# A tuned cross-network kernel: all weights kept in DRAM as 4 KB rows and loaded through the GpSimd queue

## The chip, the cores and the metric

The kernel runs on one core of one Trainium2 chip. The metric is the device time in microseconds (us). A core has TensorE (matmul), VectorE, ScalarE, GpSimd and SyncE; in the profile they are PE, DVE, ACT, POOL and SP, and "SPq" or "POOLq" is the queue of transfers that the engine issues. The profile counts 16 DMA engines for the core, and gives the time of each queue's packets as a share of all 16: in the kernel before 49.0% for q1, the queue of SyncE, and 14.4% for q0, that of GpSimd.

## The reference

```python
B, Din, L = 16384, 1024, 6            # x0 [B, 1024], ws [6, 1024, 1024], bs [6, 1024], bf16
def reference(x0, ws, bs):
    x = x0
    for l in range(L):
        x = x0 * (x @ ws[l] + bs[l]) + x      # written with einsum in the original
    return x
```

## The kernel before

The batch is cut into 8 passes (`lp`) of 2048 rows. A pass runs the 6 layers, and each layer runs two lanes of 1024 rows, so there are 96 "units" of one pass, one layer and one lane. While TensorE works on one lane, VectorE prepares the other. The product of a unit is computed with a seven-product (Strassen-like) scheme on quarters of the matrices, which needs sums of weight quarters. Pass 0 builds those sums on VectorE and saves them in a DRAM tile `Lc`; passes 1 to 7 load nine 512 KB weight tiles per layer into a ring of ten, six from `Lc` (a 4 KB row per partition) and three from the input `ws` (1 KB rows). That makes 7 x 6 x 9 = 378 loads, 252 from `Lc` and 126 from `ws`.

Activations are held transposed. So at a pass boundary three kinds of transfer meet, for each of four quarters of each lane: `x0L` of the next pass is loaded by a DMA transpose from DRAM, the result `xf` goes through a DMA transpose in SBUF back to row order (into `xL`), and `xL` is stored. In the kernel before, these and all the weight loads are issued by SyncE, on one queue.

```python
RING = 10
CIDX = {5: 0, 6: 1, 7: 2, 3: 3, "2i": 4, "4i": 5}
Lc = dram.tile([L, len(CIDX), P, KH * H], BF16, name="Lc")

def w_src(l, pid):                       # where a weight tile [128, 4, 512] comes from
    wl = ws[l]
    if pid == 1:
        return wl[0:H, 0:H].rearrange("(k p) e -> p k e", p=P)
    ...                                  # pid 2 and 4: other quarters of ws
    return Lc[l, CIDX[pid]].rearrange("p (k e) -> p k e", k=KH)

def prefetch():                          # called at every step; loads as far as ring slots are free
    while st["next"] < len(keys) and can_alloc(st["next"]):
        key = keys[st["next"]]
        if key[0] == 0 and key[2] not in (1, 2, 4):
            return
        t_ = alloc_next(key)
        st["dma"] = nc.sync.dma_start(t_[:], w_src(key[1], key[2]))

def combo(l, pid):                       # pass 0 only
    ...
    nc.sync.dma_start(Lc[l, CIDX[pid]].rearrange("p (k e) -> p k e", k=KH), t_[:])

def load_x0(lp, lane, eh, n):
    r0 = lp * LB + lane * PR + n * NB
    nc.sync.dma_start_transpose(out=q(x0L[lane], eh, n), in_=x0[r0:r0 + NB, eh * H:(eh + 1) * H])

def store_quarter(lp, lane, eh, n, xf):
    ...
    nc.sync.dma_start_transpose(out=dst, in_=xf[:].rearrange("r j k p -> r (j k p)"))
    nc.sync.dma_start(out[r0:r0 + NB, eh * H:(eh + 1) * H].rearrange("(j p) d -> p j d", p=P),
                      q(xL[lane], eh, n).rearrange("p j d -> p j d"))

def x_out(c, eh, n):
    if last_layer:
        xf = late["xf"].tile([P, KH, KH, P], BF16, name="xf")      # a pool of two buffers
        tt(xf[:]..., c..., q(xst, eh, n)..., ADD)                  # VectorE, cut
        store_quarter(lp, lane, eh, n, xf)
    elif l > 0:
        nc.gpsimd.dma_start(q(xst, eh, n), c, accum_op=ADD)
    else:
        tt(q(xst, eh, n), c, q(x0T, eh, n), ADD)

def finish(c, add, eh, n):
    tt(c, c, add, ADD)
    tt(c, c, q(x0T, eh, n), MULT)
    if nxt_x0:                                     # last layer, and a next pass exists
        load_x0(lp + 1, lane, eh, n)
    x_out(c, eh, n)
```

The `xf` pool has two buffers, so the third `xf` on VectorE must wait until the transpose of the first has landed. And the ring's slots come free in units of lane 1, so the nine loads for the first layers of the next pass are issued during the last unit of a pass, just when the boundary's transposes run.

## Time and profile before

| | before |
|---|---|
| time, median of 3 runs (range) | 2414.31 us (2412.28 to 2418.68) |
| span of the profiled run, mean granted clock | 2414.6 us, 0.983 |
| a unit inside a pass, TensorE without a gap | 23.38 us |
| the first three units of a pass, over 3 x 23.38 us (mean of seven) | 17.2 us |

The last row was worked out from the trace: a unit starts where ScalarE first evicts its P1 product. Seven boundaries of 17.2 us are 120 us, the largest loss in a kernel whose TensorE is otherwise full.

The page's busy time (busy us, share of the span, instructions), and the shares of the chain that ended last:

```profile
PE 2286.9 (95%) x12912; PEld 1269.5 (53%) x12912; DVE 2116.1 (88%) x2096; ACT 1783.9 (74%) x2485; POOL 110.7 (5%) x133
...
PE 77%; DVE 15%; DMA 5%; SPq 1%; issue 1%; ACT 1%; DVEq 0%; ACTq 0%
```

The transfers of before, from the page (out<-in, queue, kind, count, KB each, median us from issue to landing):

```profile
wp<-Lc SPq DMA_DIRECT2D x252, 512.0 KB, 4.6
wp<-in_ws_dram SPq DMA_DIRECT2D x139, 512.0 KB, 5.9
...
x0L<-in_x_dram SPq DMA_TRANSPOSE x64, 5.4
```

The waits of before (engine and line, what it waited for: us in total, times, longest):

```profile
DVE xf L63 <- DMA xL<-xf: 95.4, 21, 8.6
...
PE XB L259 <- DMA wp<-Lc: 45.5, 12, 5.9
PE XB L259 <- DMA wp<-in_ws_dram: 18.3, 7, 7.8
```

TensorE's waits for weights are the inviting target. The chain of waits tells another story. Here is the third boundary of before (start us, us, what), which has no weight load in it:

```profile
917.36 2.30 DVE D L63
...
919.69 1.24 DVE xf L63
920.93 2.49 SPq L150
...
923.52 5.08 DMA xL<-xf
928.60 0.02 issue
928.62 1.22 DVE xf L63
929.85 0.08 DVE Q L63
929.92 7.32 DMA x0L<-in_x_dram
...
951.98 1.02 PE XA L247 x4
```

VectorE's multiply at 917.36 frees `x0L` of lane 1; the transposes into it are issued only at 929.92, because the sync queue is still busy. That queue's own timeline of before shows with what:

```profile
917.10 0.46 SPq L100 DMA_DIRECT2D wp<-in_ws_dram  x1
917.65 5.76 SPq L150 DMA_TRANSPOSE x0L<-in_x_dram  x1
923.52 3.04 SPq L155 DMA_TRANSPOSE xL<-xf  x1
926.68 0.98 SPq L100 DMA_DIRECT2D wp<-Lc  x2
928.62 0.39 SPq L156 DMA_DIRECT2D out_dram<-xL  x1
929.43 0.39 SPq L100 DMA_DIRECT2D wp<-in_ws_dram  x1
929.92 6.67 SPq L150 DMA_TRANSPOSE x0L<-in_x_dram  x2
```

And the stretches around this boundary, with busy time of each engine, granted clock, DMA share and GB/s:

```profile
core 0: us, PE busy (x) PEld busy (x) DVE busy (x) ACT busy (x) POOL busy (x), PEclk, DMA share, GB/s
885.00:905.00 20.00, 20.00 (x118) 11.35 (x116) 12.25 (x11) 15.75 (x23) 0.00 (x0) 1.00 1.06 201
905.00:925.00 20.00, 14.45 (x75) 7.28 (x74) 15.61 (x18) 9.99 (x14) 0.00 (x0) 0.91 1.18 294
925.00:945.00 20.00, 14.81 (x78) 7.96 (x76) 13.33 (x14) 10.36 (x15) 0.00 (x0) 0.83 1.05 261
```

### The profile page before, as it was taken

What the parts mean: (1) busy time and instruction counts of PE and PEld (TensorE: products, weight loads), DVE (VectorE), ACT (ScalarE), POOL (GpSimd) and SP (SyncE); (2) the same over time, 40 slices, a digit from 0 to 9 for tenths busy, and PEclk for the clock granted to TensorE, in tenths of its full rate; (3) what the DMA queues carried; (4) which work ended last, traced back from release to release, by engine and by line L of the source; (5) the groups of instructions that cost most, each with busy time, mean ns of one, the idle gap of its engine ahead of it and who ended that gap; (6) DMA issues with size and microseconds to landing.
All of it is one profiled execution on the core that took longest, in us unless ns stands there. A gap on an engine that the chain in (4) does not pass through costs nothing.

```text
span 2414.6 us, 32963 instructions
## 1 busy us (share of the span) xinstructions
PE 2286.9 (95%) x12912; PEld 1269.5 (53%) x12912; DVE 2116.1 (88%) x2096; ACT 1783.9 (74%) x2485; POOL 110.7 (5%) x133
## 2 busy tenths in 40 slices
PE   6999989999899997999989999899998999989997
PEld 3454545555455554555545555455554555545553
DVE  6998879998899988999879998799987999889997
ACT  4777767777677785787767887677776878768775
POOL 0000000000000000000000000000000000000000
PEclk9999999999999999999999999999999999999998
DMA  7465695557954579545784558845588456874566
GB/s 200 137 188 136 161 236 139 148 131 179 240 150 126 135 183 237 147 122 147 191 230 130 131 149 197 218 126 131 153 201 222 114 136 165 208 197 123 147 172 144
DMA packets 439899, 400.10 MB, mean 166 GB/s; under 512 B 276416, under 2 KB 386496, under 8 KB 439744
## 3 DMA queue, kind: packets, MB, share of 16 engines
q1 hardware_dynamic: 421312, 330.89, 49.0%
q0 software_dynamic: 18432, 67.12, 14.4%
q8 instruction: 101, 1.65, 0.3%
q14 instruction: 54, 0.44, 0.1%
HBM read 211.29 MB, written 52.43 MB: 109 GB/s over the span
## 4 chain that ended last, share of the span: by engine, by line
PE 77%; DVE 15%; DMA 5%; SPq 1%; issue 1%; ACT 1%; DVEq 0%; ACTq 0%
PE pA L247 35%; PE XA L247 23%; PE XB L259 19%; DVE t L63 4%; DVE D L63 3%; DVE ti L63 3%; DMA xL<-xf 3%; DMA x0L<-in_x_dram 2%; DVE S L63 2%; SPq L150 1%; DVE xf L63 1%; DVE xL L63 1%; DVE Q L63 1%; ACT P5s L239 1%; DMA wp<-in_ws_dram 0%
## 5 line engine op out<-in xcount | busy, mean ns | idle before, releaser
L247 PEld LDWEIGHTS <-wp 128*128 128x128 bf16 x7712 | 759.0, 99 | 773.8 <-issue 46.6
L247 PE MATMUL pA<-t,wp 128*128 128x512 bf16 x3104 | 780.2, 381 | 0.0
L259 PEld LDWEIGHTS <-wp 128*128 128x128 bf16 x5040 | 494.9, 99 | 333.8 <-DMA wp<-Lc 51.3
L239 ACT CAST F<-XB 128x1024 bf16<-128x1024 f32 x360 | 364.3, 1012 | 291.0 <-PE XB L259 284.4
L259 PE MATMUL XB<-ti,wp 128*128 128x256 bf16 x2880 | 436.9, 275 | 52.4 <-DMA wp<-Lc 45.5
L247 PE MATMUL XA<-t,wp 128*128 128x512 bf16 x1536 | 400.6, 385 | 2.4 <-DMA wp<-Lc 2.4
L247 PE MATMUL XA<-xL,wp 128*128 128x512 bf16 x1280 | 326.8, 379 | 2.3 <-ACT P5s L239 2.3
L247 PE MATMUL pA<-xL,wp 128*128 128x512 bf16 x1280 | 328.5, 379 | 0.0
L242 ACT ACTIVATE U3s<-pA,b_all 128x512 bf16<-128x512 f32 x384 | 264.4, 688 | 39.4 <-PE pA L247 19.0
L239 ACT CAST G<-XB 128x512 bf16<-128x512 f32 x360 | 211.7, 588 | 106.5 <-PE XB L259 105.2
L242 ACT ACTIVATE P1s<-pA,b_all 128x512 bf16<-128x512 f32 x384 | 266.0, 693 | 26.3 <-PE pA L247 18.5
L242 ACT ACTIVATE U2s<-pA,b_all 128x512 bf16<-128x512 f32 x384 | 266.1, 693 | 14.4 <-PE pA L247 5.1
L239 ACT CAST S<-XA 128x1024 bf16<-128x1024 f32 x192 | 194.3, 1012 | 64.1 <-PE XA L247 64.1
L239 ACT CAST P5s<-XA 128x1024 bf16<-128x1024 f32 x192 | 195.3, 1017 | 50.1 <-DVE D L63 30.8
L63 DVE TENSOR_TENSOR D<-D,x0L 128x4096 bf16<-128x4096 bf16 x96 | 220.0, 2292 | 13.3 <-ACT D L242 9.4
L63 DVE TENSOR_TENSOR t<-xL 128x4096 bf16<-128x4096 bf16 x80 | 183.4, 2293 | 23.4 <-DMA xL<-S 14.7
L63 DVE TENSOR_TENSOR t<-xL,t 128x2048 bf16<-128x2048 bf16 x160 | 194.9, 1218 | 0.0
L63 DVE TENSOR_TENSOR xL<-D,xL 128x4096 bf16<-128x4096 bf16 x64 | 146.7, 2292 | 6.6
L63 DVE TENSOR_TENSOR S<-S,U2s 128x2048 bf16<-128x2048 bf16 x96 | 117.2, 1221 | 31.8 <-ACT S L239 31.5
L305 POOL DMA_DIRECT2D xL<-Q x64 | 55.2, 863 | 1905.9 <-ACT U3s L242 862.2
L259 PE MATMUL XB<-t,wp 128*128 128x256 bf16 x1008 | 139.3, 275 | 0.0
L63 DVE TENSOR_TENSOR D<-P5s,U3s 128x2048 bf16<-128x2048 bf16 x96 | 117.3, 1222 | 24.4 <-ACT U3s L242 24.4
(43 smaller groups left out, 1752.0 us busy)
## 6 DMA issues: line engine op xcount, KB each, us to landing
wp<-Lc SPq DMA_DIRECT2D x252, 512.0 KB, 4.6
wp<-in_ws_dram SPq DMA_DIRECT2D x139, 512.0 KB, 5.9
xL<-Q POOLq DMA_DIRECT2D x64, 512.0 KB, 5.7
xL<-S POOLq DMA_DIRECT2D x64, 512.0 KB, 6.4
out_dram<-xL SPq DMA_DIRECT2D x64, 512.0 KB, 3.8
Lc<-wp SPq DMA_DIRECT2D x36, 512.0 KB, 5.0
w<-in_ws_dram SPq DMA_DIRECT2D x12, 512.0 KB, 7.7
x0L<-in_x_dram SPq DMA_TRANSPOSE x64, 5.4
```

What stands on the lines that cost most here:

```text
L63: return nc.vector.tensor_tensor(out=out, in0=in0, in1=in1, op=op)
L150: nc.sync.dma_start_transpose(out=q(x0L[lane], eh, n), in_=x0[r0:r0 + NB, eh * H:(eh + 1) * H])
L239: nc.scalar.copy(out=dst, in_=src)
L242: nc.scalar.activation(out=dst, in_=src, func=IDENT, bias=bias_col(eh, m), scale=1.0)
L247: nc.tensor.matmul(dst, lhsT=w_[:, k, m * P:(m + 1) * P], rhs=b_[:, k, :], start=(start and k == 0), stop=(k == KH - 1), skip_group_check= ...
L259: nc.tensor.matmul(dst[:, m * NQ:(m + 1) * NQ], lhsT=wv[:, k, m * P:(m + 1) * P], rhs=b_[:, k, :], start=(start and m == 0 and k == 0), st ...
L305: nc.gpsimd.dma_start(q(xst, eh, n), c, accum_op=ADD)
```

## The change

The intent: the sync queue should carry only input and output. All nine weight tiles of a layer are kept in DRAM in the load's own layout, one 4 KB row per partition, and passes 1 to 7 load them through GpSimd's queue, which has little else to do (POOL is busy 5% of the span before). Pass 0 gains 18 saves. The whole diff, with context cut:

```diff
-    CIDX = {5: 0, 6: 1, 7: 2, 3: 3, "2i": 4, "4i": 5}
+    CIDX = {5: 0, 6: 1, 7: 2, 3: 3, "2i": 4, "4i": 5, 1: 6, 2: 7, 4: 8}
     Lc = dram.tile([L, len(CIDX), P, KH * H], BF16, name="Lc")
 ...
-        return Lc[l, CIDX[pid]].rearrange("p (k e) -> p k e", k=KH)
+        raise KeyError(pid)
+
+    def w_save(l, pid, t_):
+        nc.sync.dma_start(Lc[l, CIDX[pid]], t_[:].rearrange("p k e -> p (k e)"))
 ...
             t_ = alloc_next(key)
-            st["dma"] = nc.sync.dma_start(t_[:], w_src(key[1], key[2]))
+            if key[0] == 0:
+                nc.sync.dma_start(t_[:], w_src(key[1], key[2]))
+                if key[2] in (1, 2):
+                    w_save(key[1], key[2], t_)
+            else:
+                nc.gpsimd.dma_start(t_[:].rearrange("p k e -> p (k e)"), Lc[key[1], CIDX[key[2]]])
 ...
         nc.sync.dma_start(w22[l][:], w_src(l, 4))
+        w_save(l, 4, w22[l])
 ...
-        nc.sync.dma_start(Lc[l, CIDX[pid]].rearrange("p (k e) -> p k e", k=KH), t_[:])
+        w_save(l, pid, t_)
 ...
     t_ = alloc_next((0, 0, 1))
     nc.sync.dma_start(t_[:], w_src(0, 1))
+    w_save(0, 1, t_)
```

## The prediction

> **What bounds the kernel now.** TensorE is busy 2286.9 of 2414.6 us (page, part 1). By the timeline, a layer-and-lane unit inside a batch pass takes exactly 23.38 us without a TensorE gap; two hold 44.4 us of VectorE work (windows). The 96 units would so take about 2250 us; the rest is the start (first matmul at 11.1 us), the tail (about 17 us) and seven pass boundaries, each about 17 us over (first unit 35 to 39 us, second 24 to 28, third 24.1).
>
> At a boundary TensorE's visible gaps are mostly waits for weights, about 10 us each time, then 0.4 to 3.4 us for P5s, and the granted clock falls to 0.5 for 3.4 to 13.7 us. [...] But the chain of waits gives weight loads 0%. At 903 us it runs: VectorE 902.8 to 919.7 without a gap; then the x0 transposes for lane 1, whose input is free at 919.7, are issued only at 929.9, because SyncE is still issuing an earlier transpose (5.8 us), then a result transpose, weights, and a store that waits for a landing; x0 lands at 937.3; VectorE to 950.7; P5s; TensorE at 952.0. So weight waits lie mostly in the shadow of the SyncE/VectorE chain.
>
> **What changes.** TensorE, VectorE, ScalarE keep their order. 378 weight loads (252 from Lc, 126 from ws) move to GpSimd; SyncE loses them, gains 18 saves. GpSimd issues cost 0.86 us each (measured on its accumulates): no limit. 1 KB rows become 4 KB rows, but 512 KB takes each of the 16 engines 1.66 us in 1 KB packets (52 ns) and 1.6 us in 4 KB (199 ns): almost nothing. [...] the trace shows them at a share of 1.0 or more from 885 to 945 us. Bandwidth is not gained, only order.
>
> - Boundary gain: weights are issued when a slot frees (887 to 904 us) instead of 903 to 930. Weight gaps go. Lane 1's x0 transposes issue about 8 to 10 us earlier.
> - Loss there: up to six weight loads (1.6 us each) now compete with the transposes of 885 to 905 us, which hold VectorE (6.0 us wait): estimated 3 us later.
> - Net 7 us a boundary, 49 in all.
> - Start: the saves of the first two weights wait for landings (4.9, 6.3 us) ahead of the x0 transposes issued at 2.3: plus 5 us.
> - Mid-pass: [...] VectorE waits only 0.4 us for these accumulates. Unchanged.
>
> **Prediction: 2370 us** (-1.8%), range 2330 to 2420. Faster by over 2%: 0.42; within 2%: 0.54; slower: 0.04.
>
> **Right or wrong by:** waits of TensorE for weights from about 70 us to under 15; stretches at clock 0.5 mostly gone; first unit of a pass near 30 us, with waits for P5s or x0 in place of weights; wait of lane 1's x0 transposes after their input is free from 10 us to about 2; first matmul near 14 us; inner units still 23.38.
>
> **What would make it wrong:** the transposes slowed far more by competing weights (no gain); accumulates delayed behind weights so that VectorE falls behind in every unit (slower); or a chain that shortens fully, towards 2300.

The forecast's sum: 49 us won at the boundaries less 5 us lost at the start is 44 us, from 2414 to 2370.

## The result, and the profile after

| | before | after |
|---|---|---|
| time, median (range), 4 runs each | 2413.72 us (2412.28 to 2418.68) | 2509.32 us (2500.48 to 2515.29) |
| ratio of fast runs, 95% interval | | 1.0389 (1.0352 to 1.0427) |
| mean granted clock of the profiled run | 0.983 | 0.957 |

A ratio is the mean time of one kernel's fast runs over that of the other's fast runs of the same rounds, so it is not quite the ratio of the medians quoted beside it. The changed kernel is 3.9% slower. It computes the right result.

The page after shows the same amount of matmul, VectorE and ScalarE work in a longer span, and more DMA in the chain:

```profile
PE 2288.3 (91%) x12912; PEld 1272.6 (51%) x12912; DVE 2115.3 (84%) x2096; ACT 1784.9 (71%) x2485; POOL 314.4 (13%) x511
...
PE 76%; DVE 13%; DMA 7%; SPq 2%; ACT 1%; issue 1%; DVEq 0%; ACTq 0%
```

The transfers after. The median of a transpose has hardly moved, which hides what happened:

```profile
wp<-Lc POOLq DMA_DIRECT2D x378, 512.0 KB, 6.2
...
x0L<-in_x_dram SPq DMA_TRANSPOSE x64, 5.2
xL<-xf SPq DMA_TRANSPOSE x64, 4.6
```

The times from issue to landing, taken one by one from the two traces:

| us to landing | before: median / 90% / longest | after: median / 90% / longest |
|---|---|---|
| x0L<-in_x_dram | 5.5 / 8.6 / 9.3 | 5.2 / 25.5 / 31.5 |
| xL<-xf | 4.5 / 5.3 / 6.2 | 4.6 / 15.3 / 24.3 |

The medians of the first table and of this one differ by 0.1 us in one place because landings are matched singly here. A tenth of the `x0L` transposes, those at boundaries, now take 25 us and more. The waits after:

```profile
DVE xf L63 <- DMA xL<-xf: 215.7, 16, 35.4
...
PE XB L269 <- DMA x0L<-in_x_dram: 91.2, 6, 23.6
...
PE XB L269 <- DVE ti L63: 56.5, 8, 14.3
PE XA L257 <- ACT P5s L249: 23.2, 9, 3.8
...
PE XB L269 <- DMA wp<-Lc: 14.4, 1, 14.4
```

By these lines the weight waits of TensorE are nearly gone, as intended. In their place it waits for `x0L` transposes and for VectorE's `ti`, which is made from them. But a wait is put down to what came last, and the loads do not land early: at this boundary the last of them and the transpose land 0.02 us apart, and the weight-load unit (PEld) waits for `wp` three times in the run, 54.6 us in all. The chain of the same boundary after is one long step:

```profile
935.30 0.86 PE pA L257 x4
...
936.18 20.40 DMA xL<-xf
...
957.82 2.28 DVE t L63
...
972.42 1.86 PE XA L257 x4
```

The sync queue of after, in the same stretch, holds nothing but transposes and stores. Here one line can cover several issues (x2):

```profile
924.46 0.38 SPq L165 DMA_DIRECT2D out_dram<-xL  x1
924.92 11.15 SPq L159 DMA_TRANSPOSE x0L<-in_x_dram  x2
936.18 20.41 SPq L164 DMA_TRANSPOSE xL<-xf  x2
```

Over the whole run a single issue of a transpose on SyncE took up to 20.6 us (median 2.8); before it was 6.7 at most (median 2.4).

And this is what GpSimd's timeline after has at that time: nine weight loads between 923.90 and 939.92, of which three are shown.

```profile
923.90 0.53 POOL L108 DMA_DIRECT2D wp<-Lc  x1 [29.30 <-PE pA L257]
925.20 0.53 POOL L108 DMA_DIRECT2D wp<-Lc  x1 [0.77 <-PE XB L269]
...
939.92 0.53 POOL L108 DMA_DIRECT2D wp<-Lc  x1 [0.34 <-PE pA L257]
```

Matched to landings: the second `x0L` transpose, issued at 929.65, landed at 954.80 (25.2 us), and the first `xf` transpose, issued at 936.18, landed at 956.58 (20.4 us). The last of the nine loads landed at 954.8. The transposes ended when the loads ended. The stretches of after (columns as before) show TensorE almost empty for 20 us while the DMA engines are counted full and move no more bytes than in the stretch ahead of it:

```profile
921.00:941.00 20.00, 19.49 (x111) 10.57 (x108) 7.34 (x7) 16.45 (x24) 4.76 (x9) 1.00 1.09 215
941.00:961.00 20.00, 1.26 (x6) 0.76 (x7) 4.29 (x4) 0.21 (x1) 0.00 (x0) 0.57 1.10 217
961.00:981.00 20.00, 16.20 (x72) 7.95 (x71) 18.30 (x21) 8.83 (x12) 0.00 (x0) 0.75 0.95 213
```

**Where the 95.6 us are.** Four measures from the traces place them:

| mean of seven boundaries, us | before | after | difference |
|---|---|---|---|
| first three units of a pass, over 3 x 23.38 | 17.2 | 30.9 | +13.7 |
| start of lane 1's first `xf` on VectorE, after the start of the last unit | 18.5 | 42.8 | +24.3 |
| VectorE's wait just ahead of it, for an `xL<-xf` transpose | 5.3 | 29.5 | +24.2 |
| from that `xf` to the landing of lane 1's last x0 transpose | 37.9 | 26.2 | -11.7 |

Seven times 13.7 us is 96 us, the loss (the start adds 1.7 us; the two profiled runs themselves differ by 98.6). Units inside a pass are 23.38 us in both. So two things happened at each boundary. The part that the change was made for seems to come out as hoped: 11.7 us were won from lane 1's `xf` on. But 24.3 us were lost ahead of it, waiting for the transposes of lane 0. The two are not independent: by the time of lane 1's `xf` the loads had all landed, and in h1 below, where the delay is gone and the loads run beside lane 1's transposes, the 11.7 us are gone too. TensorE's idle time also went with a lower granted clock: up to the last matmul, 64.9 us at half clock before, 198.0 us after.

### The profile page after: what moved, and what is told of

Same layout as the page of the kernel before. It is cut to its first block, busy times and chain, and to the rows that moved or that the text cites. A ratio compares the mean times of both kernels' runs of the same rounds, so it can differ in the third digit from the quotient of the medians.

```text
span 2513.2 us, 33038 instructions
## 1 busy us (share of the span) xinstructions
PE 2288.3 (91%) x12912; PEld 1272.6 (51%) x12912; DVE 2115.3 (84%) x2096; ACT 1784.9 (71%) x2485; POOL 314.4 (13%) x511
## 4 chain that ended last, share of the span: by engine, by line
PE 76%; DVE 13%; DMA 7%; SPq 2%; ACT 1%; issue 1%; DVEq 0%; ACTq 0%
PE pA L257 35%; PE XA L257 23%; PE XB L269 18%; DMA xL<-xf 6%; DVE t L63 3%; DVE D L63 3%; DVE ti L63 2%; DVE S L63 2%; SPq L159 2%; DVE Q L63 1%; DVE xL L63 1%; DVE xf L63 1%; DMA x0L<-in_x_dram 0%; ACT P5s L249 0%; ACT P1s L252 0%
## 5 line engine op out<-in xcount | busy, mean ns | idle before, releaser
L108 POOL DMA_DIRECT2D wp<-Lc x378 | 219.3, 614 | 1156.3 <-PE pA L257 836.8
L63 DVE TENSOR_TENSOR xf<-Q,xL 128x2048 bf16<-128x2048 bf16 x16 | 19.6, 1225 | 206.9 <-DMA xL<-xf 206.6
```

The lines of the kernel that those rows point to most:

```text
L63: return nc.vector.tensor_tensor(out=out, in0=in0, in1=in1, op=op)
L108: nc.gpsimd.dma_start(t_[:].rearrange("p k e -> p (k e)"), Lc[key[1], CIDX[key[2]]])
```

## The experiments

The theories, with the letters that some expectations use:

- **A.** The weight loads share the DMA engines with the transposes, and another queue's packets take turns with the transposes' packets. A weight packet in the trace has 4096 bytes and takes about 159 ns, a transpose packet 256 bytes and about 18 ns. In a turn-by-turn service the transposes get little. A1: taking turns is all of it. A2: sharing also loses throughput.
- **B.** It is something special to GpSimd's queue.
- **C.** It is the order of issue alone: the loads come earlier, whatever their packets are.
- **D.** It is the layout: the 4 KB rows or the 18 saves.
- **L** (formed later, when A1 did not give the size): the sync queue feeds the 16 DMA engines in step, so the engines that also serve a foreign load set the pace for all.

### 1. e1_sync_4k: the layout alone

The changed kernel, with its loads back on the sync queue.

```diff
-                nc.gpsimd.dma_start(t_[:].rearrange("p k e -> p (k e)"), Lc[key[1], CIDX[key[2]]])
+                nc.sync.dma_start(t_[:].rearrange("p k e -> p (k e)"), Lc[key[1], CIDX[key[2]]])
```

> All weights saved as 4 KB rows as in the change, but loaded by the sync queue again. Theories: A, the DMA engines take turns packet by packet between two queues, so that a transpose of 256 B packets gets one packet through for each 4 KB packet of weights on the other queue; [...] C, the bytes of the weights merely come earlier than the transposes, whatever the queue and the packet; D, the 4 KB rows themselves are bad. A, B and C expect the time of before within 1% (2395 to 2430 us), with first units of 35 to 39 us and weight waits of TensorE near 70 us again; D expects over 2480.

Measured: 2420.73 us median against 2416.47, ratio 1.0022 (1.0005 to 1.0038). The boundary excess is 17.0 us, as before. The layout neither costs nor wins at boundaries; D is out.

### 2. e2_gp_1k: 1 KB rows on GpSimd's queue

The changed kernel, with `Lc` laid out so that a load reads 1 KB rows.

```diff
-    Lc = dram.tile([L, len(CIDX), P, KH * H], BF16, name="Lc")
+    Lc = dram.tile([L, len(CIDX), KH, P, H], BF16, name="Lc")
 ...
-        nc.sync.dma_start(Lc[l, CIDX[pid]], t_[:].rearrange("p k e -> p (k e)"))
+        nc.sync.dma_start(Lc[l, CIDX[pid]].rearrange("k p e -> p k e"), t_[:])
 ...
-                nc.gpsimd.dma_start(t_[:].rearrange("p k e -> p (k e)"), Lc[key[1], CIDX[key[2]]])
+                nc.gpsimd.dma_start(t_[:], Lc[key[1], CIDX[key[2]]].rearrange("k p e -> p k e"))
```

> The change with the saved weights laid out so that each packet is 1 KB, still on the GpSimd queue. A: a transpose packet now waits behind a 1 KB packet (46 to 52 ns) and not a 4 KB one (159), so the slowest transposes at a boundary land in about 12 us and not in 25, and the kernel takes 2430 to 2475 us. B and C expect 2495 to 2525 as the change. D expects 2400 to 2430.

Measured: 2527.66 us (2514.97 to 2551.64), ratio 1.0475 (1.0412 to 1.0539). As a test of packet size it failed, for a reason that the trace shows: GpSimd's queue has 64,768 packets of 4096 bytes, the same count as in the changed kernel. The 1 KB rows were merged into 4096-byte packets, so the packet size of the change was never altered. Its ratio is 0.9% above that of the change, but the two intervals overlap, so that it is slower than the change is not shown.

### 3. e3_gp_only: the queue alone

The kernel before, with nothing changed but the queue of the loads of passes 1 to 7.

```diff
-            st["dma"] = nc.sync.dma_start(t_[:], w_src(key[1], key[2]))
+            (nc.sync if key[0] == 0 else nc.gpsimd).dma_start(t_[:], w_src(key[1], key[2]))
```

> The queue alone: the kernel before with its weight loads of later passes on the GpSimd queue, two thirds of them in 4 KB packets and one third in 1 KB, no saves of 1, 2 and 4. A: nearly the change, 2470 to 2510 us. B and C: 2495 to 2525 less the 2 us of the start. D: 2400 to 2430.

Measured: 2504.1 us (2484.63 to 2508.65), ratio 1.0351 (1.0309 to 1.0393). The same wait as in the changed kernel appears:

```profile
DVE xf L63 <- DMA xL<-xf: 211.6, 15, 34.5
```

The queue alone gives nine tenths of the loss (3.51% of 3.89%, and the intervals overlap). With e1, the two halves of the change are told apart. One thing came with the queue: here too GpSimd's queue has 64,768 packets of 4096 bytes, so the third of the loads that comes from `ws` in 1 KB rows was merged, and the expectation's mix of packets was not what ran.

### 4. e4_act_4k: the loads on ScalarE's queue

```diff
-                nc.gpsimd.dma_start(t_[:].rearrange("p k e -> p (k e)"), Lc[key[1], CIDX[key[2]]])
+                nc.scalar.dma_start(t_[:].rearrange("p k e -> p (k e)"), Lc[key[1], CIDX[key[2]]])
```

> The change with the weight loads issued by ScalarE: another queue than the transposes', 4 KB packets[...]. A and C: as the change, 2490 to 2530 us, transposes at a boundary of 20 to 25 us. B: 2420 or less. ScalarE spends 0.3 to 0.5 us an issue, nine in two units in which it has 9 us free, so inner units should stay at 23.4 us.

Measured: 2490.86 us (2484.5 to 2492.8), ratio 1.0307 (1.0289 to 1.0324). The run is confounded, because ScalarE's evictions stood behind its issues of loads: at 1237.26 us the issue of two loads took 17.32 us, and the next eviction began at 1254.63. Two waits show what that cost; the issue of a load held ScalarE up, and with it TensorE:

```profile
ACT U3s L252 <- DMA out_dram<-xL: 74.0, 6, 17.6
...
PE XB L269 <- ACT G L249: 69.5, 6, 16.8
```

Still, transposes were slow here too: 16.7 us at the longest for `x0L`, 18.0 for `xL<-xf`. So slow transposes are not special to GpSimd's queue, which weakens B. The time itself decides nothing: the loss lies in the last unit of a pass, 42.7 to 52.6 us long instead of 23.38, where ScalarE stood.

### 5. m1_phases: bursts of transposes and loads by themselves

A micro-kernel. Its output is wrong, which doesn't matter for the time. Each phase issues a few transposes on the sync queue and as many 512 KB loads on some queue, all at once, and VectorE then waits for all of them.

```python
def tp(i):       # transpose of [512, 512] from DRAM, sync queue
    nc.sync.dma_start_transpose(out=T[i][:], in_=x0[i * NB:(i + 1) * NB, 0:H])
def w4(q, i):    # 512 KB load in 4 KB rows, on queue q (w1: 1 KB rows, w256: 256 B rows)
    q.dma_start(W[i][:], Ld[i])
for i in range(4): (tp(i), w4(gp, i))
sync_all()
for i in range(4): (tp(i), w4(sp, i))
sync_all()
...              # more phases
```

> The disputed cost by itself; wrong results on purpose, the time of the whole says nothing. Phases, each ended by a barrier, of four 512 KB transposes on the sync queue, four 512 KB loads, or both. From the kernels' traces an undisturbed transpose should take 2.2 to 2.8 us of the DMA engines and a 4 KB-row load 1.3 to 1.6, so four of each alone about 13 and 9 us with the first landing, and together, if engines lose nothing by mixing them, 17 to 20 us. C (order alone): together on two queues as long as alternating on one queue, within 2 us, whatever queue and packet. A1 (taking turns, packet by packet, without loss): the sum of both stays at 17 to 20 us, but the transposes land last, after all 4 KB loads; with 256 B rows on the other queue the transposes land earlier. A2 (transposes beside another queue lose throughput): together on two queues over 25 us, on one queue 17 to 20. B [...]: slow with GpSimd, not with ScalarE's queue. Two plain loads on two queues: no loss under any of these. The eight-and-eight phases should show the same twice as large.

Landing times from the start of the phase, from the trace:

| phase | transposes land at, us | loads land at, us |
|---|---|---|
| 4 loads, GpSimd, alone | | 3.6 to 8.3 |
| 8 transposes alone | last 20.3 | |
| 4 + 4, GpSimd 4 KB | 6.4, 11.7, 14.3, 16.2 | 4.9, 7.3, 8.8, 10.2 |
| 4 + 4, all on the sync queue, alternating | 3.8, 8.7, 12.7, 16.6 | last 18.4 |
| 4 + 4, ScalarE 4 KB | 15.0, 16.8, 18.9, 20.9 | 3.6 to 15.2 |
| 4 + 4, ScalarE 1 KB | 7.8, 12.4, 14.6, 16.5 | 4.8, 7.8, 9.6, 11.4 |
| 4 + 4, ScalarE 256 B | 7.0, 11.3, 15.4, 19.4 | 6.6, 11.1, 15.2, 19.2 |
| 4 + 4, GpSimd 1 KB rows (merged to 4096 B, as in e2) | first 8.4, last 17.1 | |
| 8 + 8, GpSimd 4 KB | 5.7, then 17.1 to 29.4 | last 16.0 |
| 8 + 8, all on the sync queue | last 34.0 | |

Transposes alone need about 2.1 us each, so nothing is lost in total: 8 + 8 takes 29.4 us on two queues and 34.0 on one. But the loads come first. In the 8 + 8 phase, while both were going, the trace counts 144 weight packets against 161 transpose packets in the 1.5 us from 246.7: nearly one to one. One for one is 4096 bytes against 256. On ScalarE's queue the landings follow the row size: with 256-byte rows both sides land together (the last at 19.4 and 19.2 us), with 4096-byte rows the first transpose lands at 15.0 us. C, order alone, cannot give this dependence on the rows; B is not needed. A1 holds for bursts and A2 does not. Three more phases fit: beside GpSimd's stores the transposes landed at 6.6 to 16.4 us; transposes within SBUF beside GpSimd's loads landed at 10.3 to 18.4; and eight plain loads on two queues took 13.7 us, about 1.7 each, so nothing was lost.

The changed kernel's trace shows the same at the boundary: 125 weight packets to 142 transpose packets in the 1.5 us from 945.5, and 124 to 140 from 947.0. Transposes alone have 1200 to 1600 packets in that time. These are the stretches with most weight packets; the others look different (see m2).

### 6. e5_store_gp: another transfer beside the transposes

The kernel before, with only the output stores on GpSimd's queue.

```diff
-        nc.sync.dma_start(out[r0:r0 + NB, eh * H:(eh + 1) * H].rearrange("(j p) d -> p j d", p=P),
+        nc.gpsimd.dma_start(out[r0:r0 + NB, eh * H:(eh + 1) * H].rearrange("(j p) d -> p j d", p=P),
```

> The kernel before, weights on the sync queue as they were, with only the output stores moved to the GpSimd queue, so that now the stores run beside transposes on another queue and the sync queue no longer waits for a landing before each store. A1 and A2: transposes beside stores get slower (landing 8 us and more where it was 4.5); the kernel takes 2430 to 2500 us. C and B with few loads: the sync queue is freed of a wait of 2 to 3 us for each of 8 stores of a boundary, so 2370 to 2410 us.

Measured: 2452.24 us against 2415.22, ratio 1.0142 (1.0123 to 1.016), boundary excess 22.4 us. (22.4 - 17.2) x 7 is 36 us, which is the loss of 37. `x0L` transposes took up to 15.4 us, 12.9 at the 90% mark, where it was 9.3 and 8.6. So it is not the weights as such: stores of the same size on another queue beside the boundary's transposes slow them too. Other kinds of transfer were not tried.

### 7. h1_hold: the loads wait for lane 0's transposes

The changed kernel, with one more dependency: the boundary's loads wait until lane 0's last `xL<-xf` transpose has landed.

```diff
+                d_ = nc.gpsimd.dma_start(t_[:].rearrange("p k e -> p (k e)"), Lc[key[1], CIDX[key[2]]])
+                if st.get("hold") is not None:
+                    tc.add_manual_dep(ins_of(d_), ins_of(st["hold"]).name, ...)
+                    if key[1] == 1:
+                        st["hold"] = None
 ...
+        d_ = nc.sync.dma_start_transpose(out=dst, in_=xf[:].rearrange("r j k p -> r (j k p)"))
+        if lane == 0 and (eh, n) == (1, 0) and lp + 1 < NLP:
+            st["hold"] = d_
```

> The change with one added wait: at a pass boundary the eight weight loads of the next pass's first layer (all but the first weight) are issued on the GpSimd queue only when the last of lane 0's result transposes has landed, so that they no longer run beside lane 0's transposes; queue, rows and bytes are the change's. Since the phases ran I hold theory A1: the engines take turns between two queues packet by packet, lose little by it, and so the queue with 4 KB packets goes first and 256 B transposes wait. A1 expects the 20 to 30 us landings of lane 0's transposes gone (under 10), first weights about 3 to 6 us late, the kernel at or under before: 2370 to 2425 us. If the loss were of another kind (saves, GpSimd's issues, DRAM rows, the accumulates in one queue with loads) this would stay at 2480 or more.

Measured: 2431.96 us (2429.27 to 2434.63) against 2413.71, ratio 1.0073 (1.0058 to 1.0088). Four fifths of the loss are gone. Lane 1's first `xf` starts 17.8 us after the last unit, where it was 42.8. It is still above the expected range, by 7 us, and the sync queue shows why: the held loads now run beside lane 1's first transposes instead.

```profile
908.86 2.84 SPq L165 DMA_TRANSPOSE x0L<-in_x_dram  x1
...
912.50 13.64 SPq L170 DMA_TRANSPOSE xL<-xf  x1
```

The second of these landed after 17.9 us. From lane 1's first `xf` to its last x0 transpose it took 39.3 us, so the 11.7 us won in the changed kernel were lost again. The boundary has transposes nearly all the time; whether the loads would cost less at another moment was not tried.

### 8. v1_late_store: the sync queue made shorter another way

The kernel before, with each output store issued one step later, so that no store waits at the head of the queue for its own transpose to land (51 waits, 68.4 us in all, in the kernel before).

```diff
+    late_store = []
+    def flush():
+        while late_store:
+            dst_, src_ = late_store.pop()
+            nc.sync.dma_start(dst_, src_)
 ...
         nc.sync.dma_start_transpose(out=dst, in_=xf[:].rearrange("r j k p -> r (j k p)"))
-        nc.sync.dma_start(out[...]..., q(xL[lane], eh, n)...)
+        flush()
+        late_store.append((out[...]..., q(xL[lane], eh, n)...))
 ...
                     store_quarter(lp, lane, 1, n, xf)
+                flush()
```

> The kernel before, weights and stores on the sync queue, but each output store is issued one step later, after the next quarter's transposes, so that the sync queue does not stand before a store waiting for the landing of the transpose that feeds it (2 to 3 us, up to eight times a boundary). If the chain of a boundary goes through the sync queue as I predicted, 3 to 5 us a boundary come off: 2380 to 2400 us. If not, 2405 to 2425.

Measured: 2404.34 us (2403.28 to 2405.49) against 2413.71, ratio 0.996 (0.9943 to 0.9976). It is the fastest kernel, though by 0.4% only. It lies between the two expected ranges, 4 us above the one and 0.7 us below the one for "if not". The boundary excess is 15.2 us instead of 17.2, and lane 1's x0 transposes are issued 7.4 us after their input is free instead of 9.7. So the boundary hangs on the sync queue in part: 2 us of it could be had without a second queue, where 3 to 5 were expected.

### 9. m2_phases: why a boundary is worse than a burst

In the bursts of m1 the loads passed quickly and little was lost. At the changed kernel's boundary a transpose took 25 us. The difference could be that the loads come spread out, as ring slots come free. So one phase has two transposes from DRAM, two in SBUF, and eight loads spaced by GpSimd's own memsets.

```python
(tp(0), tp(1), tps(2), tps(3))                 # tps: transpose SBUF to SBUF
for i in range(8): (w4(gp, i), nc.gpsimd.memset(junk[:], 0.0))     # spaced about 2.2 us
sync_all()
...                                            # the same all at once; the same on one queue
```

> Phases again, wrong results on purpose. The transposes of results read SBUF, those of x0 read DRAM; in the first phases only x0's were measured. Four SBUF transposes alone 11 to 13 us; with four 4 KB-row loads on the GpSimd queue: A1 17 to 18 us if they lose nothing, and if the slow stretches seen in the changed kernel (75 to 130 GB/s while both queues have work) come from the SBUF kind, 20 us or more; alternating on the sync queue 16 to 19. Two of each kind with eight loads on the GpSimd queue: A1 without loss 21 to 24 us; as in the kernel over 28. The same on one queue: 24 to 28, but with the first transposes landing within 5 to 12 us.

| 4 transposes and 8 loads | all landed after, us | transposes land at, us |
|---|---|---|
| the 4 transposes alone | 11.0 | |
| burst, GpSimd | 20.6 | |
| one queue (sync) | 24.2 | |
| spaced by about 2.2 us, GpSimd | 32.9 | 5.8, 15.2, 31.3, 32.9 |

The spaced phase is slower than the same work on one queue, and reproduces the boundary. Its sync queue looks like the boundary's: the issue of two transposes takes 25.39 us.

```profile
104.97 5.43 SPq L50 DMA_TRANSPOSE T<-in_x_dram  x2
110.49 25.39 SPq L53 DMA_TRANSPOSE T<-S  x2
```

From 129 to 135 us this phase has about 30 weight packets and 106 transpose packets per us. By these times an engine that alternates one of each, 159 + 18 ns, would do 5.65 of each per us. So 30 weight packets per us is an estimate of only 5.3 engines busy with weights; yet the transposes have only 106 packets per us in all, which is about what sixteen engines would have (90) if each kept to the pace of an alternating one. Ten engines that had no weights to serve should have run at full speed. They did not. This is theory L. The packets' own times show it more directly. In these 6 us the weight packets took 159 to 166 ns, but two thirds of the transpose packets took about 170 ns or 330, one or two weight packets' time, instead of 18, and some sixteen of them were under way at any moment.

The changed kernel has this too: from 951.5 to 954.5, at the end of the boundary, only 18 weight packets start, 18 x 159 ns or 2.9 us of one engine, and yet only 319 transpose packets, where transposes alone have 2400 to 3200 in 3 us. Not all of its boundary is explained by turns of packets and by L: from 938.0 to 944.0, 41 of the 143 weight packets took 0.5 to 2.1 us instead of 0.16. Why is not known, and how the 24 us divide was not worked out. That the boundary has transposes within SBUF is not the cause: four of them with four burst loads took 17.2 us, as A1 expected.

### 10. m3_few_engines: a foreign load on four engines only

To test L, four loads on ScalarE's queue use only four partitions with rows of 64 KB. In the trace they are packets of 65,536 bytes, about 8 us each, four at a time, so by inference on four of the engines. If each engine worked for itself, three quarters of the transposes' packets would flow on.

```python
def few(q, i):
    q.dma_start(X[4 * i:4 * i + 4, :], ...)    # 4 partitions x 64 KB, from ws
for i in range(4): tp(i)
for i in range(4): few(ac, i)
sync_all()
for i in range(4): w1(sp, i)                   # control: plain loads on the sync queue
for i in range(4): few(ac, i)
```

> Phases, wrong results on purpose. What the spaced phase left open is why transposes beside trickling loads lose throughput (33 us, where one queue takes 24). Theory L: the sync queue hands a transpose's packets to all 16 engines in step, so the engine with most foreign packets sets the pace of all. Here the second queue (ScalarE's) loads 1 MB into 16 partitions, four at a time, so that only some 4 of the 16 engines have foreign packets. L expects in the phase of four transposes and these loads that the 256 B packets of all engines together fall from some 800 to 1000 a us to 100 to 300 for as long as the loads last. If the engines are independent, the 12 others go on: 600 or more a us in the first 6 us, then a long tail of few packets. The loads beside plain 1 KB-row loads on the sync queue are the control.

The sync queue's line for the four transposes:

```profile
69.83 71.53 SPq L50 DMA_TRANSPOSE T<-in_x_dram  x4
```

The transpose issued at 71.2 us landed at 139.4, 68 us later, when the foreign packets were over; the next two, issued only at 101.5 and 139.0, landed at 141.5 and 143.5. The issue of the one at 71.2 took 30.2 us, of the one at 101.5 it took 37.4. While foreign packets ran (74 to 98 and 106 to 138 us), stretches of 8 us have 82 transpose packets at most, and none start from 106 to 118 us, against about 1000 per us alone. That is far under the 100 to 300 per us that L expected, beside packets of 65,536 bytes. From 106 to 134 us the long transpose packets come as two groups of exactly sixteen; all of a group took 8.05 to 8.07 us, or 8.99 to 9.01, about the time of one foreign packet. So by these counts the transpose moved in step on all engines, at the pace of those that the foreign load held, as L says. The foreign load moved some 32 GB/s in all (four times 64 KB in 8 us), where the boundaries above move over 200, so memory bandwidth did not run out.

Plain 1 KB loads on the sync queue suffered too, but far less: 121 to 147 packets per 2 us beside the foreign load against 473 to 534 without, so about a quarter was left; four held engines of sixteen would by themselves leave three quarters. So with plain loads too the sync queue slows by more than the held engines' share, but only a transpose nearly stops; what part of that is the queue's and what part the transpose's own was not separated. Three limits: the packet records do not name the engine, so "in step" is read from counts and times; the foreign load ran on ScalarE's queue, not on GpSimd's as in the kernel; and this kernel's phases leaked into each other, so the phase times are not used.

### 11. g1_boundary_sync: only the boundary's loads go back

The changed kernel, with the nine loads that are issued in the last unit of a pass back on the sync queue. The other 45 of each pass stay on GpSimd's.

```diff
-                nc.gpsimd.dma_start(t_[:].rearrange("p k e -> p (k e)"), Lc[key[1], CIDX[key[2]]])
+                last_unit = (key[1] == 0 and key[2] != 1) or key[1:] == (1, 1)
+                (nc.sync if last_unit else nc.gpsimd).dma_start(t_[:].rearrange("p k e -> p (k e)"), Lc[key[1], CIDX[key[2]]])
```

> The change, with only the nine weight loads that fall beside a boundary's transposes given back to the sync queue; the other five sixths of the loads stay on the GpSimd queue in 4 KB rows. The theory (loads on another queue beside transposes) expects all of the loss gone: 2405 to 2425 us, inner units at 23.38 us. If GpSimd's queue cost something in the rest of a pass, more than 2440.

Measured: 2414.33 us (2409.99 to 2415.54) against 2415.43, ratio 0.9994 (0.9979 to 1.0009), excess 16.7 us. VectorE's wait is back to that of before:

```profile
DVE xf L63 <- DMA xL<-xf: 93.0, 20, 7.9
```

The whole loss belongs to the nine loads beside the boundary's transposes. Mid-pass, where there are no transposes, GpSimd's queue costs nothing and wins nothing: with the other 45 loads of each pass on it the ratio is 0.9994.

### 12. v2_sp_order: v1 with the sync queue in program order

```diff
-    ctx.enter_context(tc.manual_schedule(engines={nc.tensor.engine, nc.scalar.engine, nc.vector.engine}))
+    ctx.enter_context(tc.manual_schedule(engines={nc.tensor.engine, nc.scalar.engine, nc.vector.engine, nc.sync.engine}))
```

> The kernel before with late stores, and the sync queue in program order in place of the scheduler's: at a boundary the weight loads are then issued three after each quarter's transposes, up to 10 us sooner (after 903 and 908 us in place of 914 and 927), still in one queue with the transposes. If one queue shares the engines without loss, the remaining weight waits (about 10 us a boundary) shrink: 2370 to 2395 us. If early weights delay the transposes on one queue too, 2400 to 2420.

Measured: 2410.42 us (2408.82 to 2412.79) against 2415.43, ratio 0.9981 (0.9964 to 0.9997). It missed 2370 to 2395 and lies in the range for "early weights delay the transposes on one queue too", but for a mixed reason: pass 0 lost 9.5 us against v1 (it has units of 36.01 and 29.90 us), while the boundary excess is 14.7 us, 0.5 better than v1's, and the first unit of a pass still took 35 to 38 us. v1 stays the best.

## Why the prediction was wrong

The prediction was 2370 us in a range of 2330 to 2420; measured were 2509.32 us. It gave "slower" 4%.

**The step that failed** is the second term of the boundary sum: six weight loads "now compete with the transposes of 885 to 905 us, which hold VectorE (6.0 us wait): estimated 3 us later". Measured, lane 1's first `xf` came 24.3 us later. The mechanism was named, and even listed under what would make the prediction wrong, but its size reads as if DMA engines shared by bytes: a load takes 1.6 us of engine time, so a transpose would lose a little of that (how 3 us came of it is not written down). The runs show two other things in its place. The packets of the two queues went nearly one for one, a 256-byte transpose packet for a 4096-byte weight packet (144 weight to 161 transpose packets in 1.5 us of m1, 125 to 142 in the changed kernel). And transposes slowed on all engines at once, as read from counts: beside foreign packets of about 8 us in m3 their long packets came in groups of sixteen that took 8.05 to 8.07 us, or 8.99 to 9.01, and beside loads that came one after another in m2 the last of four landed at 32.9 us, where the burst took 20.6. The turns alone would not give the size: in a burst the same work loses nothing in total (8 + 8 in 29.4 us, against 34.0 on one queue).

Point by point:

- "Bandwidth is not gained, only order": right as to bytes (a mean of 166 GB/s before, 163 after). But the order also includes who gets the next packet, and 125 weight packets to 142 transpose packets in 1.5 us gave nearly all of the bytes to the weights. The step from competing loads to "3 us later" was the author's estimate, and was the error.
- "Lane 1's x0 transposes issue about 8 to 10 us earlier": right, counted from when their input is free (wait of 9.7 us before, 1.0 after, where about 2 was predicted). From lane 1's `xf` to the landing of its last x0 transpose the time fell by 11.7 us.
- "Net 7 us a boundary" won: it was 13.7 us lost. The two measured terms, 24.3 - 11.7 = 12.6 us, give 88 us over seven boundaries; the remaining 1.1 us a boundary was not located. By the sum alone, the measured gain and the estimated loss of 3 us would have won some 60 us. But h1 shows that the gain does not stay when the loss is removed, so this sum of two separate terms was itself too simple.
- Waits of TensorE for weights "from about 70 us to under 15": right by the number, 14.4 us (and 7.5 us in pass 0). But the loads still land late; their waits are hidden behind the transposes, which land as late or later.
- "First unit of a pass near 30 us": wrong. It took 46.7 to 59.6 us, where it was 35.4 to 38.9 before.
- "Stretches at clock 0.5 mostly gone": wrong. They went from 64.9 to 198.0 us, while TensorE's waits for `x0L` came to 91.2 us, up to 23.6 at one time.
- First matmul near 14 us, start 5 us later: the first matmul moved from 11.1 to 12.8 us. The cost of the saves was overestimated.
- Layout "almost nothing": right (e1). Inner units 23.38 us, mid-pass unchanged: right, and g1 confirms it.
- "Waits for P5s or x0 in place of weights": right in kind. It was mostly x0, and far more of it than the prediction allowed.

What is shown by intervention: the queue and not the layout (e1, e3), the boundary's loads and not the others (g1), and their coincidence with transposes (h1, e5). What is read from packet counts and times: that a transpose moves in step on the 16 engines (m3, groups of exactly sixteen). That a spaced load is on only some engines at a time is the estimate of m2 (5.3 engines) and was not shown, nor how the 24 us divide between the turns of packets, the step of all engines and the long weight packets.

## What to carry to other kernels

Before moving a bulk transfer to a second queue, look at what small-packet traffic, above all DMA transposes, runs at that moment on the first: the order of issue protected it on one queue (`x0L` transposes landed after 9.3 us at the longest), while on two queues it got about one small packet per large one (142 to 125) and landed after up to 31.5 us. Mid-pass, where no transposes ran beside the loads, moving them cost nothing (g1, ratio 0.9994); where transposes hold the chain, keep the bulk loads behind them on the same queue and shorten that queue in other ways, such as a store that does not wait at its head. And look at the 90% mark of a transfer's landing time at the stage that matters, since here the medians did not move (5.5 and 5.2 us) while the boundary's transposes became three to five times slower.
